# A two-layer attention and gMLP kernel whose instruction order is planned in Python: new priorities, PE transposes, GELU in two ordered halves, scores filled during GELU

## The chip, the cores and the metric

The kernel runs on one core of a Trainium2 chip. The metric is the device time of one execution in microseconds. The core has five engines that each run their own instruction stream in order and meet only at semaphores: TensorE (PE), ScalarE (ACT), VectorE (DVE), GpSimd (POOL) and SyncE (SP), which here only issues DMAs. A wait in a stream holds everything behind it in that stream.

## What is computed

One sequence of S = 2048 tokens of width D = 512 goes twice through two residual blocks:

```python
x = A_x
x = x + A(layernorm(x));  x = x + B(layernorm(x))     # layer 0
x = x + A(layernorm(x));  x = x + B(layernorm(x))     # layer 1, same weights

def A(x):                       # 32 query heads of 16, one shared key/value head
    q = (x @ wq) as 32 heads of 16;  k = x @ wk;  v = x @ wv
    p = softmax(q @ k.T * 16 ** -0.5)
    return (p @ v, heads side by side) @ wo

def B(x):                       # gMLP: F = 1792, half of it 896
    z = gelu(x @ w_in)                       # tanh approximation
    z1, z2 = z[:, :896], layernorm(z[:, 896:])
    g = w_sp @ z2 + b_sp[:, None]            # mixes over the 2048 positions
    return (z1 * g) @ w_out
```

B needs z2 of all positions before its last sum over positions is complete, and layer 1 needs keys and values of all positions of layer 0. So each layer ends in a stretch in which no softmax work is left to fill the engines.

## The kernel before

**Blocks and units.** The softmax exponentials are the bulk: 2 layers x 2048 blocks of 128 keys x 512 (query, head) columns. Query tokens are taken in six chunks, `chunks = [512, 512, 512, 256, 128, 128]`. A group is 512 (query, head) columns for four sets of heads; a unit is a group and one tile of 128 keys, and it has four blocks. PE makes a block's scores (line 1615), ScalarE or VectorE takes the exponential, and PE multiplies the result with the values and adds over the 16 units of a group (line 1419), strictly unit after unit.

**Two engines for the exponential.** ScalarE takes blocks in activations of three and two (line 1343) from a ring of five PSUM banks, `ring = [(0, 3), (3, 2)]`: `FillStream` refills one part of the ring while ScalarE reads the other. VectorE takes single blocks from two further PSUM banks, the side banks 5 and 7, which all other matmul work shares. `DexStream.take` picks such a block at least `LOOK = 6` units ahead of the fill, if a side bank is free and VectorE's queue holds at most `BACKLOG = 3.0` us. Its first operation (line 1520) reads the bank; when two blocks are together, `chain` runs six more (lines 1547 to 1558) and writes the result `Pd`. `PVStream` cannot pass a unit before all its four blocks are done, and the 15 slots of `Pa` that ScalarE writes come free only as `PVStream` goes on.

**The planner.** `Sched` is a list scheduler that runs in Python before anything is built. Each operation has an engine, a modelled duration, dependencies and a priority (a lower number goes first). At each step the engine that can start soonest commits the ready operation of the best priority, and the order of commits becomes the fixed order of that engine's instructions. Streams (fill 0.0, PV 0.5, warm matmuls) compete with ordinary operations. A `job` is matmul work that holds a side bank from its first piece until its readers are done. On the chip the order stays; only the moments differ from the plan.

**The rest of the work.** When a chunk's attention is done, `finish_group` normalises it, `project` transposes it (by DMA, or on PE for the last chunk) and multiplies it with `wo`, `ln` normalises the rows, and `mixer_chunk` computes z1 and z2, stages both without GELU, and then runs GELU on whole staged tiles, so that ScalarE changes its function table twice per batch and not twice per tile. Chunks 0 and 1 share one such batch; 2, 3 and 4 have their own; the last chunk takes GELU straight from PSUM. After GELU come the statistics of z2 (line 1013), an inverse root on GpSimd (1019) and the normalisation (1023).

**Spatial passes.** `passes = [(0, 8, 1), (8, 12, 2), (12, 15, 4)]`: the sum over positions is taken in three passes of 28 jobs (line 1088) as soon as chunks 1, 2 and 4 are through, added into `gp` by VectorE (1100, 1101). The last of these is called the early pass below. The last tile of positions is added in `closing`, which also multiplies by z1 and by `w_out`, and in layer 0 makes the keys of layer 1.

**Warm matmuls.** `WarmStream` issues matmuls of zeros (line 1601) where the planned matmul work in a window of time is small. They wait for nothing but their zero tile and, at times, a bank.

Of the kernel before, what the change touches and what calls it, by code (L numbers as in the profile page):

```python
# [19 lines left out]
FH = 896  # L20
NF = 7
# [11 lines left out]
class Op:  # L33
    __slots__ = ("eng", "fn", "dur", "deps", "prio", "seq", "start", "end", "vis", "sem", "val",
                 "clock", "job", "first", "nun", "users", "ready", "alts", "table", "lat", "dma", "at_commit", "cols", "slow")
# [22 lines left out]
class Sched:  # L58
# [3 lines left out]
    def __init__(self, side_banks):  # L62
# [10 lines left out]
        self.exp_next = None  # L73
        self.tick = {}
# [40 lines left out]
    def op(self, eng, fn, dur, deps=(), prio=5.0, sem=None, job=None, first=False, alts=(), table=None,  # L115
# [28 lines left out]
        o.at_commit = None  # L144
        o.nun = 0
# [20 lines left out]
    def _pick(self, eng):  # L166
# [3 lines left out]
        for o in self.ready[eng]:  # L170
# [8 lines left out]
            if r < INF:  # L179
                cands.append((r, o.prio, o.seq, o, 0.0))  # L180
# [39 lines left out]
    def commit(self, o, t, eng=None):  # L220
# [36 lines left out]
        if o.dma:  # L257
            self.dma_free = max(self.dma_free, o.end) + o.dma / 240e3
            o.vis = self.dma_free + 1.9
# [20 lines left out]
    def job(self, pieces, cons, deps, prio, sem="side", piece_deps=None, soft=()):  # L280
# [3 lines left out]
        for i, (fn, dur) in enumerate(pieces):  # L284
            dd = list(deps) if i == 0 else [prev]
            if piece_deps is not None:
                dd += piece_deps[i]
            prev = self.op("pe", (lambda e, fn=fn: fn(e, j.bank.idx)), dur, dd, prio if i == 0 else min(prio, CONT), sem=sem, job=j,
                           cols=dur * 1900.0, first=(i == 0), soft=[d for c in cons for d in c.get("deps", ())] + list(soft) if i == 0 else ())
        outs = []  # L290
# [74 lines left out]
LOOK = 6  # L365
BACKLOG = 3.0
# [47 lines left out]
class Kern:  # L414
    def __init__(self, nc, A_x, A_wq, A_wk, A_wv, A_wo, B_x, B_w_in, B_w_sp, B_b_sp, B_w_out, out):
# [10 lines left out]
        self.passes = [(0, 8, 1), (8, 12, 2), (12, 15, 4)]  # L426
        self.s_fin = 15
# [79 lines left out]
        sc.streams["pe"] = [self.fill_s, self.pv_s, WarmStream(self)]  # L507
        sc.streams["act"] = [self.exp_s]
        sc.exp_next = self.exp_s.next_time
        self.units = []  # L510
# [23 lines left out]
    def transpose(self, out, src, deps, sem, pr):  # L534
        return self.dma(lambda e: e.dma_start_transpose(out, src), deps, sem, 131072, pr, issue=1.25)
# [265 lines left out]
    def finish_group(self, g, pv_last):  # L801
# [19 lines left out]
        def nm(h, e, b):  # L821
# [16 lines left out]
            [ev, self.c_id], 1.2)  # L838
# [11 lines left out]
    def project(self, g, norms):  # L850
# [7 lines left out]
        for h in range((nq + 1) // 2):  # L858
# [16 lines left out]
            if g.ci < len(self.chunks) - 1:  # L875
# [8 lines left out]
                norms + [self.c_id], 1.3)  # L884
# [4 lines left out]
        for qt in range(nq):  # L889
            t = g.t0 // 128 + qt  # L890

            def pe(e, b, qt=qt):
# [7 lines left out]
                dur=d_psum(512), prio=0.8, deps=[self.x_op[t]])], [evs[qt], self.l_wo], 1.4)  # L900
# [5 lines left out]
    def mixer_chunk(self, g):  # L906
# [5 lines left out]
        pr = PR_LAST if last else (PR_SMALL if g.ci >= 3 else 3.0)  # L912
        evs = []
        war = list(self.xnTB_read)
        for i in range(0, nt, 2):
            ts = T[i:i + 2]
            evs += self.ln(ts, lambda t: [self.x_op[t]], self.xnTB[:, i:i + len(ts), :, :], war, pr, last)
# [29 lines left out]
        elif g.ci == 0:  # L947

            z1v = self.gp[:, 0].bitcast(BF16)
            z1_war = [o for f in range(NF) for o in self.gp_read[(0, f)]]  # L950
        else:
            z1v = self.z1s[:].rearrange("p (f t) -> p f t", f=NF)[:, :, 0:n]
            z1_war = list(self.z1s_free)
# [26 lines left out]
        if g.ci == 0:  # L980
            self.held = (T, z1, z2, z1v)
            return
        zs = [(T[0], n, z1v)]
        if g.ci == 1:
            T, z1, z2 = [a + b for a, b in zip(self.held[:3], (T, z1, z2))]
            zs = [(T[0], n, self.held[3])] + zs
# [4 lines left out]
        def gl(e):  # L991
            for (_t, _n, v) in zs:
                e.activation(v, v, ACTF.Gelu_apprx_tanh)
# [4 lines left out]
        else:  # L998
            gs = z1 = [sc.op("act", gl, d_gelu(NF * nt * 128) + d_gelu(nt * FH), z1 + z2, -1.0, table="gelu")] * (2 * nt)
        for (zt, zn, v) in zs:  # L1000
# [5 lines left out]
            elif zt == 0:  # L1006
                for f in range(NF):
                    self.gp_read[(0, f)] = [sp]
            else:
                self.z1s_free = [sp]  # L1010
# [21 lines left out]

    z2_op = {}
    z2_read = {}
    z1_spill = []
    gp_ops = {}
    gp_read = {}


    def spatial(self, s0, s1, layer):  # L1040
        sc = self.sc
        acc = s0 > 0
        pr = 2.5 if acc else 4.0
        nst = s1 - s0
        early = s1 == self.s_fin
        z2f = self.z2n[:].rearrange("p t f -> p (t f)")
# [18 lines left out]
        nsl = 1 if nst > 4 else 2  # L1065
        for tc in range(4):
            if early:
                w_, ld, held = self.wsP[tc]
            else:
                sl = tc % nsl  # L1070
                w_ = wsl[:, 2048 * sl:2048 * sl + 512 * nst].rearrange("p (s t) -> p s t", s=nst)
                ld = self.dma(lambda e, w_=w_, tc=tc: e.dma_start(w_, self.ws_dv[:, s0:s1, tc * 512:(tc + 1) * 512]),
# [595 lines left out]
```

## Time and profile before

| | |
|---|---|
| median of 8 runs | 1869.98 us (1869.2 to 1872.5) |
| the profiled execution | 1869.83 us, of which the span of instructions is 1868.0 us |
| granted TensorE clock, mean | 0.99 |
| ScalarE busy | 1756.3 us (94% of the span) |
| VectorE busy | 1737.8 us (93%) |
| TensorE busy | 1581.5 us (85%) |
| first exponential of layer 0, last | 14.4 us, 880.6 us |
| last exponential of layer 1 | 1813.0 us |

Times in the profile are microseconds from the start of the span. In a timeline, a row gives start, length, engine, line, operation, tiles, the number of instructions merged into the row, and in brackets the idle time of the engine before it and what ended it. Instructions of one engine overlap a little, so lengths can add up to more than the span.

### The profile page before, as it was taken

What the parts mean: (1) busy time and instruction counts of PE and PEld (TensorE: products, weight loads), DVE (VectorE), ACT (ScalarE), POOL (GpSimd) and SP (SyncE); (2) the same over time, 40 slices, a digit from 0 to 9 for tenths busy, and PEclk for the clock granted to TensorE, in tenths of its full rate; (3) what the DMA queues carried; (4) which work ended last, traced back from release to release, by engine and by line L of the source; (5) the groups of instructions that cost most, each with busy time, mean ns of one, the idle gap of its engine ahead of it and who ended that gap; (6) DMA issues with size and microseconds to landing.
All of it is one profiled execution on the core that took longest, in us unless ns stands there. A gap on an engine that the chain in (4) does not pass through costs nothing.

```text
span 1868.0 us, 30304 instructions
## 1 busy us (share of the span) xinstructions
PE 1581.5 (85%) x11807; PEld 477.6 (26%) x11889; DVE 1737.8 (93%) x3107; ACT 1756.3 (94%) x1581; POOL 53.3 (3%) x94
## 2 busy tenths in 40 slices
PE   8777788778879888989887788887788798998888
PEld 3222222212222222223432122222222222222234
DVE  8999999999889999996889999999999689989978
ACT  8999999999989999998579999999999899999983
POOL 2000000000000000000100000000000000000000
PEclk9999999999999999999999999999999899999999
DMA  9700010000010020221210000000000100111213
GB/s 276 192 1 1 12 35 1 1 1 18 7 40 24 23 46 1 66 72 46 66 33 1 1 1 12 10 26 1 5 14 7 40 24 24 46 43 35 62 45 110
DMA packets 125142, 68.58 MB, mean 37 GB/s; under 512 B 79172, under 2 KB 121416, under 8 KB 125000
## 3 DMA queue, kind: packets, MB, share of 16 engines
q1 hardware_dynamic: 123416, 66.48, 13.2%
q8 instruction: 95, 1.56, 0.3%
q14 instruction: 47, 0.39, 0.1%
q10 hardware_dynamic: 1584, 0.16, 0.1%
HBM read 30.97 MB, written 17.83 MB: 26 GB/s over the span
## 4 chain that ended last, share of the span: by engine, by line
ACT 38%; DVE 27%; PE 18%; issue 15%; POOL 1%; ACTq 0%; POOLq 0%; DVEq 0%
ACT Pa L1343 36%; PE ps_all L1088 5%; PE ps_all L1615 5%; DVE E L1520 4%; DVE Pd L1558 4%; PE ps_all L1419 3%; DVE E L1553 2%; DVE E L1556 2%; DVE E L1547 2%; PE ps_all L1177 2%; DVE gp L1100 2%; DVE st L622 1%; DVE z2n L937 1%; DVE E L1550 1%; DVE E L1549 1%
## 5 line engine op out<-in xcount | busy, mean ns | idle before, releaser
L1343 ACT ACTIVATE Pa<-ps_all 128x1536 bf16<-128x1536 f32 (+1 forms) x1439 | 1637.2, 1371 | 31.8 <-PE ps_all L1615 17.0
L1615 PE MATMUL ps_all<-qs,kT 32*128 32x512 bf16 x4096 | 566.1, 387 | 229.9 <-ACT Pa L1343 207.9
L1520 DVE TENSOR_SCALAR E<-ps_all 128x512 int32<-128x512 f32 x501 | 341.8, 684 | 27.4 <-PE ps_all L1615 24.7
L1615 PEld LDWEIGHTS ps_all<-qs,kT 32*128 32x128 bf16 x4096 | 139.4, 91 | 778.2 <-ACT Pa L1343 726.4
L1419 PE MATMUL ps_all<-Pa,V 128*32 128x512 bf16 x3595 | 325.1, 388 | 1.5 <-DVE Pd L1558 0.6
L1558 DVE SCALAR_TENSOR_TENSOR Pd<-E 128x1024 uint16<-128x1024 int32 x251 | 304.9, 1215 | 1.1
L1601 PE MATMUL ps_all<-zero 128*128 128x512 bf16 x817 | 262.7, 393 | 2.5 <-POOL zero L585 1.0
L1088 PE MATMUL ps_all<-wsT,z2n 128*128 128x512 bf16 x659 | 185.5, 382 | 12.6 <-issue 3.8
L1419 PE MATMUL ps_all<-Pd,V 128*32 128x512 bf16 x501 | 177.7, 389 | 0.0
L1553 DVE TENSOR_TENSOR E<-E 128x1024 f16<-128x1024 f16 x251 | 171.7, 684 | 3.4
L1556 DVE TENSOR_TENSOR E<-E 128x1024 f16<-128x1024 f16 x251 | 171.4, 683 | 2.5
L1547 DVE TENSOR_SCALAR E<-E 128x1024 f16<-128x1024 uint16 x251 | 171.5, 684 | 1.6
L1549 DVE TENSOR_SCALAR E<-E 128x1024 f16<-128x1024 f16 x251 | 105.0, 418 | 2.2
L1550 DVE TENSOR_SCALAR E<-E 128x1024 f16<-128x1024 f16 x251 | 104.6, 417 | 2.3
L1601 PEld LDWEIGHTS ps_all<-zero 128*128 128x128 bf16 x817 | 62.8, 98 | 138.7 <-issue 116.9
L1419 PEld LDWEIGHTS ps_all<-Pa,V 128*32 128x32 bf16 x3595 | 65.4, 94 | 125.1 <-issue 113.8
L1100 DVE TENSOR_TENSOR gp<-ps_all,gp 128x512 f16<-128x512 f32 x112 | 75.1, 683 | 23.2 <-PE ps_all L1088 21.8
L1088 PEld LDWEIGHTS ps_all<-wsT,z2n 128*128 128x128 bf16 x714 | 54.5, 97 | 105.2 <-issue 54.7
L784 PE MATMUL ps_all<-xnTA,wq_pad 128*128 128x512 bf16 (+2 forms) x384 | 72.4, 313 | 2.0 <-DVE qs L793 1.3
L962 PE MATMUL ps_all<-xnTB,w_in_r 128*128 128x512 bf16 (+2 forms) x336 | 62.6, 310 | 5.2 <-DVE z1s L973 2.3
L926 PE MATMUL ps_all<-w_in_r,xnTB 128*128 128x448 bf16 x256 | 63.4, 356 | 3.7 <-DVE z2n L937 1.4
L1013 DVE BATCH_NORM_STATS2 st<-z2n 128x6 f32<-128x448 bf16 x64 | 36.2, 602 | 22.1 <-ACT z2n L994 18.9
(87 smaller groups left out, 1028.3 us busy)
## 6 DMA issues: line engine op xcount, KB each, us to landing
wsT_scratch<-gp SPq DMA_DIRECT2D x16, 512.0 KB, 3.6
wsT<-wsT_scratch SPq DMA_DIRECT2D x8, 1024.0 KB, 5.4
z1s<-z_scratch SPq DMA_DIRECT2D x16, 448.0 KB, 3.8
wsT<-wsT_scratch SPq DMA_DIRECT2D x8, 512.0 KB, 3.4
z_scratch<-z1s SPq DMA_DIRECT2D x4, 896.0 KB, 5.2
X<-in_A_x_dram SPq DMA_DIRECT2D x8, 256.0 KB, 5.6
out_dram<-X SPq DMA_DIRECT2D x16, 128.0 KB, 1.9
w_in_r<-in_B_w_in_dram SPq DMA_DIRECT2D x1, 1792.0 KB, 10.6
```

Of the source, the lines that this page charges most:

```text
L1088: ins = e.matmul(self.b32(b), self.z2n[:, s, f * 128:(f + 1) * 128], w_[:, s - s0, :], start=st, stop=sp)
L1343: return e.activation(k.Pa[:, base:base + n, :], k.b32(b0, n).rearrange("p (k q) -> p k q", k=n), ACTF.Exp, scale=SCALE)
L1419: ins = e.matmul(k.b32(k.pvb)[32 * j:32 * j + 32, :], k.V[:, u.kt, 32 * j:32 * j + 32], b.slot, tile_position=(0, 32 * j), start=u.first, ...
L1520: return k.sc.op("dve", lambda e: e.tensor_scalar(k.eI[:, s, 512 * i:512 * (i + 1)], k.b32(j.bank.idx)[:, 0:512], C_LOG2, C_BIAS, op0=ALU. ...
L1547: return lambda e: e.tensor_scalar(out, a, m, None, op0=ALU.mult)
L1549: return lambda e: e.tensor_scalar(out, a, b, None, op0=ALU.add)
L1550: return lambda e: e.tensor_scalar(out, a, m, b, op0=ALU.mult, op1=ALU.add)
L1553: o4 = sc.op("dve", lambda e: e.tensor_tensor(q, u, w, ALU.mult), d_sb(n, 0.521e-3), [o3], pr)
L1556: o6 = sc.op("dve", lambda e: e.tensor_tensor(q, q, u, ALU.mult), d_sb(n, 0.521e-3), [o5], pr)
L1558: o7 = sc.op("dve", lambda e: e.scalar_tensor_tensor(po.bitcast(U16), I, 2.0 ** -9, q, op0=ALU.mult, op1=ALU.add), d_sb(n, 1.042e-3), [o6] ...
L1601: return e.matmul(k.b32(k.pvb if b is None else b.idx), k.zero[:], k.zero[:, None, :].to_broadcast([P, 4, P]), start=b is not None, stop=b ...
L1615: return e.matmul(self.b32(bank), self.kT[32 * j:32 * j + 32, kt * 128:(kt + 1) * 128], self.qs[32 * j:32 * j + 32, g.q.slot, :], tile_pos ...
```

## The change

1. **Near units first on VectorE.** Operations of VectorE's exponentials carry their unit. If it is less than `NEAR = 4` units ahead of the PV stream, the planner gives them priority 0.1 in place of 2.0 or 2.8.
2. **Spatial.** The early pass gets priority 1.6 (was 2.5), below the 2.0 of `closing`; the adds of a pass never go under 1.0. While one of its jobs waits for its start, `take` gives VectorE no block. `take` also holds back where free side banks would not be enough for waiting jobs of priority under `URGENT = 1.0`. (A split load for passes of more than eight tiles is added too, which the passes here do not use.)
3. **Chunks 3 to 5.** Their transposes and projection get priority 0.9 (were 1.2 to 1.4). For chunk 4 the two DMA transposes (of the attention output and of the normalised rows) become PE transposes with a copy out of PSUM; the last chunk did so already.
4. **GELU.** Chunks 3 and 4 share one batch. In each batch z2 is done first, as its own operation, and z1 after it; the statistics of z2 wait for the first alone, the spill of z1 to DRAM for the second.
5. **`SoloStream`.** A new PE stream at priority 0.4: when both parts of the ring are full and ScalarE is busy for at least 1.2 us more, it makes a single score block for VectorE.
6. **Warm matmuls** that the plan sets after a gap of more than 0.3 us on PE get a wait for the latest ScalarE or VectorE operation that the plan has finished in the 1.5 us before.
7. **Model.** A DMA transpose is planned with 1.2 us of issue and 0.9 us of latency (were 1.25 and 1.9).

```diff
+NEAR = 4
+URGENT = 1.0
+        self.gelus = [(0, 1), (2,), (3, 4), (5,)]
-        sc.streams["pe"] = [self.fill_s, self.pv_s, WarmStream(self)]
+        sc.streams["pe"] = [self.fill_s, self.pv_s, SoloStream(self), WarmStream(self)]
+        sc.unit_now = lambda: self.pv_s.u
...
@@ Sched._pick
-                cands.append((r, o.prio, o.seq, o, 0.0))
+                late = o.unit is not None and o.unit < self.unit_now() + NEAR
+                cands.append((r, 0.1 if late else o.prio, o.seq, o, 0.0))
...
@@ Kern.transpose
-        return self.dma(lambda e: e.dma_start_transpose(out, src), deps, sem, 131072, pr, issue=1.25)
+        return self.sc.op("sp", lambda e: e.dma_start_transpose(out, src), 1.2, deps, pr, sem=sem, dma=131072, lat=0.9)
...
@@ finish_group, project
-            [ev, self.c_id], 1.2)
+            [ev, self.c_id], 0.9 if g.ci >= 3 else 1.2)
-            if g.ci < len(self.chunks) - 1:
+            if g.ci < 4:
-                norms + [self.c_id], 1.3)
+                norms + [self.c_id], 0.9 if g.ci >= 3 else 1.3)
-                dur=d_psum(512), prio=0.8, deps=[self.x_op[t]])], [evs[qt], self.l_wo], 1.4)
+                dur=d_psum(512), prio=0.8, deps=[self.x_op[t]])], [evs[qt], self.l_wo], 0.9 if g.ci >= 3 else 1.4)
...
@@ mixer_chunk
-            evs += self.ln(ts, lambda t: [self.x_op[t]], self.xnTB[:, i:i + len(ts), :, :], war, pr, last)
+            evs += self.ln(ts, lambda t: [self.x_op[t]], self.xnTB[:, i:i + len(ts), :, :], war, pr, last, g.ci == 4)
...
-        def gl(e):
+        def gl1(e):
+            ins = None
             for (_t, _n, v) in zs:
-                e.activation(v, v, ACTF.Gelu_apprx_tanh)
+                ins = e.activation(v, v, ACTF.Gelu_apprx_tanh)
+            return ins
+
+        def gl2(e):
             return e.activation(z2f[:, t0 * FH:(t0 + nt) * FH], z2f[:, t0 * FH:(t0 + nt) * FH], ACTF.Gelu_apprx_tanh)
...
-            gs = z1 = [sc.op("act", gl, d_gelu(NF * nt * 128) + d_gelu(nt * FH), z1 + z2, -1.0, table="gelu")] * (2 * nt)
+            gs = [sc.op("act", gl2, d_gelu(nt * FH), z1 + z2, -1.0, table="gelu")] * (2 * nt)
+            z1 = [sc.op("act", gl1, sum(d_gelu(NF * zn) for _t, zn, _v in zs), z1 + z2, -0.9, table="gelu")]
...
@@ spatial
-        pr = 2.5 if acc else 4.0
+        pr = 1.6 if early else 2.5 if acc else 4.0
...
-                    fn=ev_fn, dur=d_psum(512), prio=pr - 1.5,
+                    fn=ev_fn, dur=d_psum(512), prio=max(1.0, pr - 1.5),
...
+                if early:
+                    self.early_first.append(sc.first_op)
...
@@ DexStream.take
+        if any(o.start is None and o.ready is not None and o.ready <= t for o in k.early_first):
+            return None
+        want = sum(o.first and o.prio < URGENT and o.ready <= t for o in sc.ready["pe"])
+        if want and sum(not b.busy and not b.closed and b.free_at <= t for b in sc.banks) <= want:
+            return None
...
@@ SoloStream.peek
+            t = max(f, sc.bank_free())
+            if not all(k.fill_s.pending) or t == INF or sc.free["act"] < t + 1.2:
+                return None
+            self.x = k.dx_s.take(t, ())
...
+        return (max(f, sc.bank_free(), max(d.vis for d in self.deps)), 0.4)
...
@@ WarmStream.commit
-        o = k.sc.op("pe", fn, 512 / 2400.0, [k.c_zero] + (b.rel if b is not None else []), 9.0, sem="warm")
+        pace = []
+        if t > k.sc.free["pe"] + 0.3:
+            pace = [d for en in ("act", "dve") for d in k.sc.order[en][-8:] if t - 1.5 < d.vis <= t]
+            pace = sorted(pace, key=lambda d: -d.vis)[:1]
+        o = k.sc.op("pe", fn, 512 / 2400.0, [k.c_zero] + pace + (b.rel if b is not None else []), 9.0, sem="warm")
```

## The prediction

> **What bounds it now.** I read the page's busy times and groups first, then ScalarE's own waits, then the timeline around the places where those waits are.
>
> ```profile
> PE 1581.5 (85%) x11807; PEld 477.6 (26%) x11889; DVE 1737.8 (93%) x3107; ACT 1756.3 (94%) x1581; POOL 53.3 (3%) x94
> ...
> L1343 ACT ACTIVATE Pa<-ps_all 128x1536 bf16<-128x1536 f32 (+1 forms) x1439 | 1637.2, 1371 | 31.8 <-PE ps_all L1615 17.0
> ...
> L1520 DVE TENSOR_SCALAR E<-ps_all 128x512 int32<-128x512 f32 x501 | 341.8, 684 | 27.4 <-PE ps_all L1615 24.7
> ```
>
> ScalarE and VectorE share the exponentials and both are nearly full. VectorE does 501 of the 4096 blocks, ScalarE 3595, in 1637.2 us: 0.455 us a block, and that is the price of any block that goes from one to the other. A VectorE block costs 0.684 us for line 1520 and half of a chain (0.684 + 0.418 + 0.684 + 0.417 + 0.683 + 1.215 = 4.10 us): 2.73 us. In windows of 25 us, ScalarE is busy all 25 of 25 through nearly all of 100 to 500 and 975 to 1440: nothing can be gained there unless VectorE takes more. What remains is ScalarE's idle time (112 us) and its work other than exponentials (119 us). Its waits, in total, times and longest:
>
> ```profile
> ACT Pa L1343 <- PE ps_all L1615: 17.0, 41, 1.3
> ACT xnTB L662 <- PE ps_all L654: 13.3, 2, 6.8
> ACT Pa L1343 <- PE ps_all L1419: 13.3, 5, 6.6
> ```
>
> The third is the odd one: exponentials that wait for the PV matmuls, so for free slots of Pa. ScalarE's timeline shows where:
>
> ```profile
> 503.70 1.28 ACT L993 ACT_TABLE_LOAD   x1
> 504.99 3.19 ACT L993 ACTIVATE gp<-gp 128x3584 bf16<-128x3584 bf16 x1
> 508.09 3.17 ACT L993 ACTIVATE z1s<-z1s 128x3584 bf16<-128x3584 bf16 x1
> 511.17 6.16 ACT L994 ACTIVATE z2n<-z2n 128x7168 bf16<-128x7168 bf16 x1
> 517.35 1.28 ACT L1343 ACT_TABLE_LOAD   x1
> 518.64 5.61 ACT L1343 ACTIVATE Pa<-ps_all 128x1024 bf16<-128x1024 f32 x5
> ...
> 538.99 3.28 ACT L1343 ACTIVATE Pa<-ps_all 128x1024 bf16<-128x1024 f32 x3 [3.93 <-PE ps_all L1419]
> ```
>
> and VectorE's timeline over the same stretch why:
>
> ```profile
> 506.67 1.22 DVE L1558 SCALAR_TENSOR_TENSOR Pd<-E 128x1024 uint16<-128x1024 int32 x1
> 517.36 1.68 DVE L1013 BATCH_NORM_STATS2 st<-z2n 128x6 f32<-128x448 bf16 x3 [9.47 <-ACT z2n L994]
> ...
> 533.08 3.47 DVE L1023 TENSOR_SCALAR z2n<-z2n,mv,rs 128x896 bf16<-128x896 bf16 x8 [0.77 <-POOL rs L1019]
> ...
> 539.99 1.23 DVE L1558 SCALAR_TENSOR_TENSOR Pd<-E 128x1024 uint16<-128x1024 int32 x1
> ```
>
> VectorE runs dry for 9.47 us while ScalarE does GELU, z1 first; then statistics and normalisation (priority 2.7 and 2.5) go ahead of the chain (2.8) whose first block was read at 520.4. Its Pd comes after 537.7, the PV matmuls stand until then, and ScalarE stands 3.93 us. Layer 1 repeats it: 9.40 us dry, then 6.59 us of ScalarE at 1477. PE shows the third part:
>
> ```profile
> 504.61 7.30 PE L1601 MATMUL ps_all<-zero 128*128 128x512 bf16 x33
> 519.72 0.61 PE L1615 MATMUL ps_all<-qs,kT 32*128 32x512 bf16 x3 [7.82 <-ACT Pa L1343]
> ```
>
> The 33 warm matmuls, which wait for nothing, run at once; PE then idles 7.82 us, and from 519.7 to 523.9 the granted clock is 0.52, a matmul 0.61 us in place of 0.39.
>
> **The change, term by term** (both layers; minus is time saved).
>
> *A. Waits after the large GELU.* In layer 0 ScalarE idles 0.33 + 3.93 + 0.58 us after it, in layer 1 0.77 + 0.50 + 6.59 + 0.21: 12.9 us, of which 10.5 are the two PV waits. Near-first lifts the chain to 0.1 when its unit is within four of PV. Four units are 16 blocks, some 14 of them ScalarE's, 6.4 us by 0.455; a chain needs 4.1 us plus one operation in its way, so it comes in time. Statistics also start when the z2 half ends, 6.2 us sooner. The stall goes to bn_stats and line 1023, later by a chain of 4.1 us each; behind them waits pass 0, whose adds run until 753, so nothing is late by it. I take 9.5 of the PV waits and 1 of the 2.4 us that the slow clock causes (pacing): **-10.5** (between -5, if the split alone helps, and -12.9).
>
> *B. One GELU batch fewer a layer.* It removes two table loads a layer. A load is 1.28 us, and the next exponential starts 0.01 us after it ends (517.35 + 1.28 against 518.64): 4 x 1.28 = **-5.1**. [...] The rows show no gap on either side of a load (the exponential before it ends at 503.68), so I keep 5.1. The GELU elements are the same, but the two tiles of chunk 3 now come between GELU and the early pass: 1.6 us more z2 GELU, four statistics at 0.60 and two normalisations at 0.51, some 5 us. Against that, chunk 4 reaches its GELU sooner (E).
>
> *C. Scores during GELU.* VectorE's two dry stretches total 18.9 us. What the earlier statistics do not use SoloStream can fill, and either way VectorE time is freed: 18.9 / 2.73 = 6.9 blocks, at 0.455 us 3.1 us. I take 5.5 blocks, since a free bank and a short queue are needed: **-2.5** (0 to -3.1).
>
> *D. After chunk 4's GELU.* ScalarE idles 1.14 us at 860 and 1.30 + 0.24 at 1795, with PE at half clock (0.61 us matmuls, mean clock 0.78 over 854 to 861). Paced warm matmuls keep the clock: **-1.5** (0 to -2.7).
>
> *E. The end of a layer.* From the last exponential to the last chunk's transposed rows:
>
> ```profile
> 880.57 1.28 ACT L1359 ACT_TABLE_LOAD   x1
> ...
> 891.61 0.60 ACT L662 ACTIVATE xnTB<-ps_all 128x512 bf16<-128x512 bf16 x1 [6.56 <-PE ps_all L654]
> ```
>
> and on VectorE between the links of that chain:
>
> ```profile
> 889.52 1.28 DVE L1100 TENSOR_TENSOR gp<-ps_all,gp 128x512 f16<-128x512 f32 x2
> 890.72 0.40 DVE L637 TENSOR_SCALAR xn<-X,mv,rs 128x512 bf16<-128x512 bf16 x1
> 891.03 1.28 DVE L1100 TENSOR_TENSOR gp<-ps_all,gp 128x512 f16<-128x512 f32 x2
> ```
>
> The adds of the early pass still run between the links. The links themselves (PV 0.6, oT 0.69, transposes 0.4, reciprocal 0.25, on 0.42, transposes 0.4, copy 0.6, four matmuls 1.04, X 0.69, statistics 0.68 + 0.17 + 0.14, root 0.6, xn 0.41, transposes 0.4) are 7.5 us, with some 0.1 us for each of 13 hand-overs 8.8. They take 11.0 here and 12.1 in layer 1 (1813.0 to 1825.1), so at most 5.5 us could go if the early pass were over by then. But from 860 to 881 PE is busy 20.3 of 21 us with no warm matmul, and 15 of 28 jobs are done: it is the matmuls that limit the pass, not a priority. It would have to start earlier. PE transposes save some 1.3 us twice (a DMA transpose lands 2.5 us after issue; four PE transposes 0.4 and the copy 0.6 with a semaphore on each side), and held-back banks some 4 us of the 18.8 that chunk 4 takes from its row of X (832.4) to GELU (851.2); the 5 us of B and a shorter attention take that back. **0** (-5.5 to +4, if the pass is that much later). [...]
>
> *F. What it costs.* take() is shut while the early pass waits, and where chunks 3 to 5 want a bank. Line 1520 has 19 blocks from 775 to 860 in layer 0 and none after; 22 from 1700 to 1793. If 8 of these 41 fall to ScalarE: 8 x 0.455 = **+3.6** (0 to +18.7). Four copies more out of PSUM, 0.6 us each, half on ScalarE: **+1.2**. And in the 17 us that A, B and D remove, VectorE would have done 501/1868 blocks a us, 4.6 in all: **+2.1**.
>
> Sum: -10.5 - 5.1 - 2.5 - 1.5 + 0 + 3.6 + 1.2 + 2.1 = -12.7. The span goes from 1868.0 to 1855.3, the execution from 1869.83 to 1857.1; the median lies 0.15 above that execution, so **1857**. This case alone runs from 1850 to 1865.
>
> **Rivals.** *Larger gain:* A in full (12.9), no block lost and E at its best: -12.7 - 2.4 - 3.6 - 5.5 = -24.2, **1846**. For it: four parts of the change aim at the banks and the chain. Against: full PE before the end. *It does not do what it says:* the side banks are always taken, SoloStream never fires, and near-first seldom decides; A falls to -5 and C to 0: -4.7, **1865**. *The gain goes to VectorE's lost share:* all 41 blocks of F move to ScalarE, +15.0 more: **1872**. VectorE's queue there is full of adds, which speaks for it; that only banks with waiting jobs are held back, against. *Slower:* the pacing waits. A paced warm matmul stands in PE's stream; if its VectorE partner is later on the chip than in the plan, the fill behind it waits, and ScalarE with it. A score matmul that waited for a VectorE bank lost 0.44 us (4.4 us over 10 times). It makes the kernel slower once 12.7 + 3.7 = 16.4 us are lost, at 37 such holds; 60 of the 817 warm matmuls give +26.4, **1883**. Against it: most steady-state gaps on PE end with ScalarE, which keeps its planned pace.
>
> **How the numbers follow.** Chances: the sum 0.52, larger gain 0.20, does not do what it says 0.08, lost share 0.10, pacing 0.10. A measurement can tell about 0.2%, 3.7 us: faster is below 1866.2, slower above 1873.7. Faster: 0.51 + 0.20 + 0.05 + 0.02 = 0.78. Same: 0.01 + 0.03 + 0.05 = 0.09. Slower: 0.03 + 0.10 = 0.13. The range for eight in ten, 1842 to 1873, holds nearly all of the first case, 0.15 of the second (E or C may give still more), 0.08 and 0.07.
>
> **What would show it.** A: no wait of line 1343 for line 1419 above 1.5 us, statistics about 6 us after GELU begins. B: 17 table loads in place of 21. C: VectorE idle under 4 us in the large GELU, and line 1520 still at 490 to 510 blocks; under 470 means the lost share. D: clock 0.95 or more right after GELU. E: still 9 to 13 us from the last exponential to the copy of xnTB. Pacing: idle time of ScalarE before line 1343 above 32 us in the steady stretches. The forecast is wrong if the new plan moves stalls to places where ScalarE was full.

## The result and the profile after

The changed kernel takes **1858.8 us** (median of 11 runs, 1853.4 to 1868.1) against 1870.95 for the kernel before (32 runs, 1869.2 to 1878.2): ratio **0.9935, interval 0.9924 to 0.9946**, faster by 0.65%. The profiled execution took 1858.5 us with a span of 1856.7; before it was 1869.83 and 1868.0, so the two spans differ by 11.3 us and can be taken apart.

The page of the changed kernel first: busy time of each engine, then its two groups of exponentials.

```profile
PE 1581.2 (85%) x11779; PEld 474.6 (26%) x11868; DVE 1735.8 (93%) x3108; ACT 1751.1 (94%) x1577; POOL 48.0 (3%) x90
...
L1371 ACT ACTIVATE Pa<-ps_all 128x1536 bf16<-128x1536 f32 (+1 forms) x1439 | 1635.8, 1367 | 24.0 <-PE ps_all L1697 22.3
...
L1554 DVE TENSOR_SCALAR E<-ps_all 128x512 int32<-128x512 f32 x500 | 340.9, 684 | 32.1 <-PE ps_all L1697 29.8
```

VectorE does 500 blocks, before it did 501; ScalarE's exponentials last 1635.8 us, before 1637.2. So the share of the engines hardly moved, and the gain is not more work on VectorE. ScalarE's idle time before exponentials fell from 31.8 to 24.0 us, and its other work by 3.8 (1751.1 - 1635.8 = 115.3, against 119.1). Its waits (engine, what it wants, whom it waits for: us in total, times, longest):

```profile
ACT Pa L1371 <- PE ps_all L1697: 22.3, 43, 3.1
ACT xnTB L671 <- PE ps_all L663: 13.7, 2, 7.0
...
ACT Pa L1371 <- PE ps_all L1447: 0.2, 1, 0.2
```

The wait for the PV matmuls (line 1447, before 1419) is gone: 0.2 us in place of 13.3. The wait for scores (line 1697, before 1615) grew from 17.0 to 22.3. The table loads, before (first two rows) and after (five more loads lie on other lines in each kernel: 21 and 17 in all):

```profile
L993 ACT ACT_TABLE_LOAD x8 | 10.3, 1283 | 0.1
L1343 ACT ACT_TABLE_LOAD x8 | 10.3, 1283 | 0.1
...
L1007 ACT ACT_TABLE_LOAD x6 | 7.7, 1283 | 0.1
L1371 ACT ACT_TABLE_LOAD x6 | 7.7, 1283 | 0.1
```

ScalarE's timeline over the large GELU of layer 0:

```profile
498.95 1.28 ACT L1007 ACT_TABLE_LOAD   x1
500.25 6.18 ACT L1007 ACTIVATE z2n<-z2n 128x7168 bf16<-128x7168 bf16 x1
506.33 3.17 ACT L1003 ACTIVATE gp<-gp 128x3584 bf16<-128x3584 bf16 x1
509.41 3.17 ACT L1003 ACTIVATE z1s<-z1s 128x3584 bf16<-128x3584 bf16 x1
512.60 1.28 ACT L1371 ACT_TABLE_LOAD   x1
513.89 12.45 ACT L1371 ACTIVATE Pa<-ps_all 128x1024 bf16<-128x1024 f32 x11
527.30 2.52 ACT L1371 ACTIVATE Pa<-ps_all 128x1536 bf16<-128x1536 f32 x2 [0.95 <-PE ps_all L1697]
530.80 10.51 ACT L1371 ACTIVATE Pa<-ps_all 128x1536 bf16<-128x1536 f32 x9 [0.98 <-PE ps_all L1697]
```

VectorE over the same stretch:

```profile
505.24 1.29 DVE L1554 TENSOR_SCALAR E<-ps_all 128x512 int32<-128x512 f32 x2 [0.31 <-PE ps_all L1697]
506.45 0.68 DVE L1591 TENSOR_TENSOR E<-E 128x1024 f16<-128x1024 f16 x1
507.05 1.67 DVE L1027 BATCH_NORM_STATS2 st<-z2n 128x6 f32<-128x448 bf16 x3
...
515.98 0.67 DVE L815 CAST oT<-ps_all 128x512 bf16<-128x512 f32 x1
...
516.69 1.17 DVE L1593 SCALAR_TENSOR_TENSOR Pd<-E 128x1024 uint16<-128x1024 int32 x1
```

Two blocks are filled during the GELU (505.24, `SoloStream`), the statistics start 6.8 us after the z2 half begins, and VectorE is idle for 0.31 us where it was 9.47. The chain's last operation, at 516.69, goes between casts and normalisations. PE shows what was left over:

```profile
512.75 1.25 PE L1679 MATMUL ps_all<-zero 128*128 128x512 bf16 x5 [0.79 <-DVE st L1027]
514.97 0.39 PE L1697 MATMUL ps_all<-qs,kT 32*128 32x512 bf16 x2 [0.97 <-ACT Pa L1371]
...
525.76 0.95 PE L1113 MATMUL ps_all<-wsT,z2n 128*128 128x512 bf16 x2
526.64 0.61 PE L1697 MATMUL ps_all<-qs,kT 32*128 32x512 bf16 x3
527.18 1.03 PE L1113 MATMUL ps_all<-wsT,z2n 128*128 128x512 bf16 x2
```

The warm matmuls now come in small groups, each behind a VectorE operation, and the scores right after the GELU run at full clock (0.39 us; clock 1.00 from 513 to 525; in the kernel before the 12 us after this GELU, 518.6 to 530.6, had 0.78). But from 525.9 PE is at half clock after all (0.61 us a score matmul, clock 0.66 from 525 to 530), just when the spatial pass puts its matmuls ahead of the scores: the two waits of 0.95 and 0.98. The largest wait for scores of the kernel, after chunk 2's GELU in layer 0, comes behind spatial matmuls too (line 1113), at the end of a half-clock stretch (clock 0.50 from 730.7 to 737.5):

```profile
739.86 5.97 ACT L1371 ACTIVATE Pa<-ps_all 128x1536 bf16<-128x1536 f32 x5 [3.15 <-PE ps_all L1697]
```

The largest after chunks 3 and 4 comes behind warm matmuls, at half clock as well (0.50 from 853.6 to 856.9); on PE:

```profile
853.00 0.39 PE L1697 MATMUL ps_all<-qs,kT 32*128 32x512 bf16 x2 [4.03 <-ACT Pa L1371]
853.33 3.40 PE L1679 MATMUL ps_all<-zero 128*128 128x512 bf16 x8
856.65 0.74 PE L1697 MATMUL ps_all<-qs,kT 32*128 32x512 bf16 x5
```

PE stood still for 4.03 us, then eight warm matmuls at 0.42 us each ran in front of the scores, and ScalarE idled 2.02 us until 857.23.

**The account of the span.** A layer's attention is counted from its first exponential to its last. Layer 0: 866.2 before, 864.7 after. Layer 1: 893.8 and 882.3. What lies around them is 1.6 us longer: -1.5 - 11.5 + 1.6 = -11.4, the 11.3 of the spans but for rounding. In the attention the parts are, both layers: idle before exponentials -7.8, table loads -5.1, exponentials -1.4, GELU -0.4, other work and its waits +1.6, which is the -13.0 of the two layers but for rounding. In layer 0 the idle time even grew (12.2 to 14.1), since scores came late elsewhere, the 3.15 us at 739.86 above all: nearly all of the gain is in layer 1.

### The profile page after: what moved, and what is told of

Same layout as the page of the kernel before. It is cut to its first block, busy times and chain, and to the rows that moved or that the text cites. A ratio compares the mean times of both kernels' runs of the same rounds, so it can differ in the third digit from the quotient of the medians.

```text
span 1856.7 us, 30131 instructions
## 1 busy us (share of the span) xinstructions
PE 1581.2 (85%) x11779; PEld 474.6 (26%) x11868; DVE 1735.8 (93%) x3108; ACT 1751.1 (94%) x1577; POOL 48.0 (3%) x90
## 4 chain that ended last, share of the span: by engine, by line
ACT 37%; DVE 25%; PE 22%; issue 14%; POOL 1%; DMA 0%; SPq 0%; ACTq 0%; POOLq 0%
ACT Pa L1371 35%; PE ps_all L1697 6%; PE ps_all L1113 5%; DVE E L1554 4%; PE ps_all L1447 4%; DVE Pd L1593 3%; DVE E L1588 2%; DVE E L1591 2%; DVE E L1582 2%; PE ps_all L1679 2%; DVE st L631 1%; PE ps_all L1205 1%; DVE E L1585 1%; DVE E L1584 1%; PE ps_all L936 1%
## 5 line engine op out<-in xcount | busy, mean ns | idle before, releaser
L1371 ACT ACTIVATE Pa<-ps_all 128x1536 bf16<-128x1536 f32 (+1 forms) x1439 | 1635.8, 1367 | 24.0 <-PE ps_all L1697 22.3
L1554 DVE TENSOR_SCALAR E<-ps_all 128x512 int32<-128x512 f32 x500 | 340.9, 684 | 32.1 <-PE ps_all L1697 29.8
L1593 DVE SCALAR_TENSOR_TENSOR Pd<-E 128x1024 uint16<-128x1024 int32 (+1 forms) x251 | 304.2, 1212 | 0.7
L1679 PE MATMUL ps_all<-zero 128*128 128x512 bf16 x780 | 258.1, 402 | 27.9 <-DVE E L1554 3.6
L1113 PE MATMUL ps_all<-wsT,z2n 128*128 128x512 bf16 x650 | 190.6, 388 | 13.3 <-issue 4.3
L1588 DVE TENSOR_TENSOR E<-E 128x1024 f16<-128x1024 f16 (+1 forms) x251 | 171.4, 683 | 3.2
L1591 DVE TENSOR_TENSOR E<-E 128x1024 f16<-128x1024 f16 (+1 forms) x251 | 171.3, 683 | 2.4
L1582 DVE TENSOR_SCALAR E<-E 128x1024 f16<-128x1024 uint16 (+1 forms) x251 | 171.4, 683 | 1.6
L1585 DVE TENSOR_SCALAR E<-E 128x1024 f16<-128x1024 f16 (+1 forms) x251 | 104.9, 418 | 2.6
L1584 DVE TENSOR_SCALAR E<-E 128x1024 f16<-128x1024 f16 (+1 forms) x251 | 104.6, 417 | 2.4
L1205 PE MATMUL ps_all<-E 128*128 128x512 bf16 x215 | 52.1, 380 | 4.2 <-ACT E L1184 1.6
```

Source lines behind the costliest of these rows:

```text
L1113: ins = e.matmul(self.b32(b), self.z2n[:, s, f * 128:(f + 1) * 128], w_[:, s - s0, :] if s - s0 < na or not spare else wsp[:, s - s0 - na, :],
L1371: return e.activation(k.Pa[:, base:base + n, :], k.b32(b0, n).rearrange("p (k q) -> p k q", k=n), ACTF.Exp, scale=SCALE)
L1554: c = k.sc.op("dve", lambda e: e.tensor_scalar(k.eI[:, s, 512 * i:512 * (i + 1)], k.b32(j.bank.idx)[:, 0:512], C_LOG2, C_BIAS, op0=ALU.mul ...
L1582: return lambda e: e.tensor_scalar(out, a, m, None, op0=ALU.mult)
L1584: return lambda e: e.tensor_scalar(out, a, b, None, op0=ALU.add)
L1585: return lambda e: e.tensor_scalar(out, a, m, b, op0=ALU.mult, op1=ALU.add)
```

## The experiments

Each was timed in 5 rounds against the kernel before on the same chip. For differences from the changed kernel I take the difference of the two ratios times 1871 us, as not all ran on one chip.

### One part taken out of the change

**Near units not lifted.** `-NEAR = 4` / `+NEAR = -100000`.

> The changed kernel with NEAR set so low that no VectorE operation is ever lifted; all else as changed. Theory of the prediction (near-first clears the two PV waits of 3.9 and 6.6 us): they come back, line 1371 waits for line 1447 for 5 to 10 us in all, and the time is 5 to 8 us above the changed kernel, some 1864 to 1867 us. Rival (the GELU order does it: with z2 first the statistics are through before the chains are needed): under 2 us above the changed kernel, no wait for line 1447 above 1.5 us.

1871.25 us, ratio 0.9999 (0.9987 to 1.0012): the whole gain is gone, 12 us, more than the theory's 5 to 8. Its waits of exponentials:

```profile
ACT Pa L1371 <- PE ps_all L1697: 23.7, 45, 3.1
ACT Pa L1371 <- PE ps_all L1447: 11.0, 3, 6.7
```

The PV waits are back at 11.0 us, with the z2 half still first. But 6.69 of them come at 655 to 662, in the spatial pass and not after the large GELU: a cast of the pass, four residual adds of a chunk (line 908), two reads of new blocks and links of a second chain come between the links of the first, which takes from 651.95 to 660.93, 9.0 us in place of the 4.1 of its own work. So the lift matters outside the large GELU too.

**z1 first again.** The two priorities of the GELU halves exchanged:

```diff
-  gs = [sc.op("act", gl2, ..., -1.0, table="gelu")] ...
-  z1 = [sc.op("act", gl1, ..., -0.9, table="gelu")]
+  gs = [sc.op("act", gl2, ..., -0.9, table="gelu")] ...
+  z1 = [sc.op("act", gl1, ..., -1.0, table="gelu")]
```

> The changed kernel with the two GELU operations of a batch the other way round, z1 first, so that the statistics of z2 wait for both again. Theory of the prediction: VectorE has some 6 us less to do in each large GELU, 2 to 3 us slower than the changed kernel, near-first still clears the PV wait. Rival (the order is the main gain): 6 to 10 us slower, with PV waits back on ScalarE.

1867.38 us, ratio 0.9980 (0.9970 to 0.9991), so 8.4 us lost, with no PV wait above 0.8 us: the size of the rival, without the PV waits that it named. Neither expectation is met.

**Chunk 3's GELU by itself.** `-gelus = [(0, 1), (2,), (3, 4), (5,)]` / `+gelus = [(0, 1), (2,), (3,), (4,), (5,)]`.

> The changed kernel with chunks 3 and 4 in GELU batches of their own again: 21 table loads, not 17. Theory of the prediction (1.28 us a load): 5.1 us slower than the changed kernel. [...] Rival (waiting for chunk 4 and the longer way to the early pass eat the loads up): within 2 us of the changed kernel or faster.

1869.27 us, ratio 0.9985 (0.9973 to 0.9997): 9.4 us lost where four loads account for 5.1. The trace shows next to nothing beside the 1.28 us of a load: in all 20 loads between other work of ScalarE the load starts 0.02 us after the instruction before it and the next starts 0.01 us after the load. The profiled execution is one of the fastest of its runs (1861.0 at a mean clock of 0.990); the changed kernel took 1853.4 and 1854.3 at that clock, so some 7 us remain.

**Warm matmuls without the wait.** `-if t > k.sc.free["pe"] + 0.3:` / `+if False:`.

> The changed kernel with warm matmuls that wait for nothing, as before. Theory of the prediction: 2 to 3 us slower, with the clock at about half for some 4 us after each large GELU. Rival 1 (the pacing waits hold fills back): faster than the changed kernel by over 3 us. Rival 2 (SoloStream's matmuls and the shorter dry stretch keep the clock already): within 1 us.

1859.08 us, ratio 0.9943 (0.9931 to 0.9955): not to be told from the changed kernel. The theory's 2 to 3 us are not there; the second rival has the time right but not the reason, since without the waits the clock is low (0.59 from 513 to 525). Without them 21 warm matmuls run in one row at 501 and PE then idles 8.28 us. The windows view (window, its length, busy time and number of instructions of each engine, granted clock, DMA) shows the clock of the changed kernel:

```profile
513.00:525.00 12.00, 8.35 (x64) 2.33 (x63) 11.46 (x27) 11.99 (x11) 3.15 (x2) 1.00 0.46 153
525.00:530.00 5.00, 5.00 (x23) 0.94 (x21) 4.00 (x8) 3.80 (x4) 0.00 (x0) 0.66 0.00 0
```

and of the one without the wait:

```profile
513.00:525.00 12.00, 10.83 (x60) 2.31 (x60) 10.30 (x25) 11.04 (x10) 3.15 (x2) 0.59 0.43 143
525.00:530.00 5.00, 4.97 (x38) 1.37 (x36) 4.93 (x10) 4.73 (x5) 0.00 (x0) 1.00 0.02 3
```

So pacing moves the half-clock stretch, but ScalarE waits no less with it: 0.95 + 0.98 = 1.93 us in the 18 us after the load, against 0.51 + 0.24 + 0.22 + 0.21 = 1.18 without.

**No filling during GELU.** `-[self.fill_s, self.pv_s, SoloStream(self), WarmStream(self)]` / `+[self.fill_s, self.pv_s, WarmStream(self)]`.

> The changed kernel without SoloStream. Theory of the prediction: VectorE's share in the large GELUs falls by about 2 blocks a layer, 1 to 2.5 us slower than the changed kernel. Rival (the lone score matmuls only move blocks that VectorE would take a little later): within 1 us.

1863.24 us, ratio 0.9953 (0.9941 to 0.9965): 3.4 us lost, a little over the theory's 1 to 2.5. VectorE still does 501 blocks, so the blocks it misses in the GELU it takes elsewhere. ScalarE's idle time before exponentials is 32.2 us in place of 24.0, of which 3.1 are waits for the PV matmuls, the longest 2.2.

**Nothing refused to VectorE, no urgent early pass.** The two early returns in `take` out, and `-pr = 1.6 if early else 2.5 if acc else 4.0` / `+pr = 2.5 if acc else 4.0`.

> The changed kernel with take() never shut for waiting jobs and the early pass at 2.5 again; the priorities 0.9 of the jobs of chunks 3 to 5 stay. Theory of the prediction (the refusals cost blocks and give nothing back): line 1554 has 505 to 510 blocks, 2 to 4 us faster than the changed kernel. Rival (the banks they keep free bring chunk 4 to its GELU sooner and the early pass with it): slower by 2 to 6 us, GELU of chunk 4 some 4 us later.

1857.22 us, ratio 0.9924 (0.9903 to 0.9944), overlapping that of the changed kernel; 505 blocks in place of 500. The refusals cost VectorE five blocks, 5 x 0.455 = 2.3 us, and in these two traces they are paid back at the end: from the last exponential to the end it took 59.0 us here, 55.5 with them. The theory's 505 blocks are there; its 2 to 4 us cannot be told from nothing.

**Chunk 4's transposes by DMA again.** `-if g.ci < 4:` / `+if g.ci < 5:`, and the fifth chunk's flag to `ln` dropped.

> The changed kernel with chunk 4's two transposes done by DMA again. Theory of the prediction (2.5 us of slack hides them): within 2 us of the changed kernel. Rival (chunk 4 is on the path to the early pass and so to the end of the layer): 3 to 5 us slower, the last exponential to xnTB over 13 us.

1868.66 us, ratio 0.9982 (0.9972 to 0.9993): 8.8 us lost, more than either expectation. Yet chunk 4 reaches its GELU no later: the load comes 35.5 us before layer 1's last exponential, in the changed kernel 33.8. VectorE has 493 blocks, and waits 42.5 us for their scores in place of 29.8; ScalarE's exponentials take 1641.0 us (+5.2) and its idle time before them is 28.5 (+4.5). Why is not shown.

Seven parts taken out one at a time cost 12.0 + 8.4 + 9.4 + 1.5 + 3.4 - 2.1 + 8.8 = 41.4 us; the whole change gained 12.2. Either the parts need one another, or each edit makes the planner write another order and pays for that too.

### An edit that means nothing

`-"dve": 0.14` / `+"dve": 0.15`, the hand-over latency that the planner counts for VectorE; once in the changed kernel, once in the kernel before.

> The changed kernel with one number of the planner altered that means nothing for the work: VectorE's hand-over latency counted as 0.15 us instead of 0.14, so that the written order of the engines differs while every rule of the change stays. Theory 1 (the leave-one-out runs are steep because each part really carries its gain): within 2 us of the changed kernel, 1857 to 1861. Theory 2 (any edit draws a new order from a spread of some 5 us, and the changed order is a good draw): 3 to 10 us slower, 1862 to 1869, with other small waits for scores after the GELUs and no PV wait above 2 us.

> The kernel before with the same meaningless number altered (0.15 for 0.14). Theory 1: within 2 us of the kernel before, and the two PV waits after the large GELU return (8 to 12 us in sum). Theory 2: 3 to 8 us away from it on either side; PV waits still there, since nothing lifts the chain over the statistics, but of another size.

Changed kernel: 1864.16 us, ratio 0.9963 (0.9950 to 0.9975), **5.2 us slower** than with 0.14. Kernel before: 1875.69, ratio 1.0022 (1.0009 to 1.0034), **4.1 slower**. Theory 2 has the times right: a new order is worth some 4 to 5 us by itself, and no difference below that says anything of a part. Its signs are missed in part: the changed kernel with 0.15 has a PV wait of 2.7 us (3.0 in all), and VectorE does 493 blocks in it too, so the transposes are not needed for that number.

The pair still differs by 1875.69 - 1864.16 = 11.5 us, as the first pair did by 12.1, so the change is faster under both orders, but not in the same way. The traces of the second pair differ by 6.0 us (spans of 1870.1 and 1864.1): the four loads give 5.1, idle time before exponentials 1.7 (29.0 and 27.3), since the PV waits that A removes are not there. And the runs of this pair have mean clocks of 0.981 and 0.990, those of the first 0.988 and 0.984. By 0.9 us for each 0.001 (last section) some 8 of the second pair's 11.5 us go with the clock, an estimate; at equal clocks it would differ by some 3 us, and the first pair by some 15. The mean clock is a part of what an order draws. What the change gains is therefore known to several us only, and what a single part gains cannot be read from its removal to better than about 5 us.

The kernel before with 0.15 holds a second surprise, in its waits:

```profile
ACT Pa L1343 <- PE ps_all L1615: 25.6, 49, 1.5
...
ACT Pa L1343 <- PE ps_all L1419: 1.6, 4, 0.8
```

Nothing lifts the chain, yet the PV waits are 1.6 us and not 13.3. VectorE's timeline in the large GELU of layer 0, first one row of the kernel before, then two of this one:

```profile
520.38 0.69 DVE L1520 TENSOR_SCALAR E<-ps_all 128x512 int32<-128x512 f32 x1
...
522.75 1.68 DVE L1013 BATCH_NORM_STATS2 st<-z2n 128x6 f32<-128x448 bf16 x3 [9.13 <-ACT z2n L994]
...
531.58 0.69 DVE L1520 TENSOR_SCALAR E<-ps_all 128x512 int32<-128x512 f32 x1 [1.53 <-PE ps_all L1615]
```

It is dry for 9.13 us as before, but its next block is first read 7.5 us after the exponentials resume (531.58 against 524.03; in the kernel before 520.38 against 518.64), so its chain was not yet needed while the statistics ran; that this is the reason is argued, the small PV waits are measured. The stall that I priced was an accident of one order. The waits for scores are 25.6 us here, 17.0 there.

### Parts alone, on the kernel before

**The lift alone**, as in the diff of the change (`unit`, `NEAR = 4`, priority 0.1), GELU in one piece. Then **the lift and the z2 half first**. Then these two and **the early pass made urgent** (`pr = 1.6 if early`, adds not under 1.0, `take` shut while it waits).

> The kernel before with the chain's lift alone, GELU still z1 first in one piece. The lift decides term A by itself: VectorE still idles 8 to 9.5 us in each large GELU, statistics start only after it, but the chain comes before them, so PV waits under 2 us and a time of 1862 to 1866. If the earlier statistics are needed too, PV waits of 3 us or more remain and the time is 1867 or above.

> The kernel before with term A alone: the chain's operations lifted when their unit is within four of PV, and the z2 half of GELU first. Nothing else of the change. My sum: -9.5 of the PV waits, less 1.2 that VectorE would have done in that time: 1862 to 1864, with PV waits under 2 us and 21 table loads. Spread theory: the PV waits go all the same, but the time lies anywhere from 1860 to 1871.

The lift alone: 1884.21 us, ratio 1.0069 (1.0057 to 1.0082), **slower than before by 13 us**, with the small PV waits of the first expectation and a time, 17 us above 1867, that only the second one's "or above" covers. With the z2 half first: 1864.34, ratio 0.9961 (0.9948 to 0.9974), faster by 7.3, close to my sum, without any PV wait. The waits of the lift alone:

```profile
ACT Pa L1348 <- PE ps_all L1625: 36.6, 65, 2.1
...
ACT Pa L1348 <- PE ps_all L1424: 0.9, 1, 0.9
```

and of both, where no wait for the PV matmuls is left:

```profile
ACT Pa L1353 <- PE ps_all L1630: 22.4, 44, 1.9
```

The lift took 12.4 us of PV waits away in the first, and waits for scores took 19.6 more. VectorE is still dry for 8.42 us in the large GELU of layer 0 and has its statistics to do afterwards, only later; that this other work, which empties PSUM, is what keeps the scores waiting is argued, not shown. With the statistics under the GELU the same lift leaves 22.4. Of the 14.2 us by which its span is longer (1882.2), 8.4 lie behind the last exponential; and the mean clock of its runs is 0.979 against 0.988 before, some 8 us by the slope of the last section. The two accounts overlap.

But the second does not give what its attention gives. Layer 1 is shorter by 13.8 us (880.0 against 893.8), and then the time from the last exponential to the end is 63.0 us in place of 55.0. On PE, at the end:

```profile
1839.77 0.59 PE L1098 MATMUL ps_all<-z2n 128*128 128x512 bf16 x2
1840.20 2.75 PE L1098 MATMUL ps_all<-wsT,z2n 128*128 128x512 bf16 x12
1843.34 3.20 PE L1187 MATMUL ps_all<-E 128*128 128x512 bf16 x14 [0.39 <-DVE gp L1110]
...
1851.59 2.11 PE L1098 MATMUL ps_all<-wsT,z2n 128*128 128x512 bf16 x9
```

Matmuls of the spatial passes (line 1098) stand between those of `closing` 40 to 54 us after the last exponential, and ScalarE idles 13.27 us there. Of the passes' adds 32 were left at the last exponential, before 14, and came due at the end. VectorE had taken 510 blocks, nine more than before; that they put the adds off is argued.

> The kernel before with the chain's lift, the z2 half first, and the early pass made urgent (priority 1.6, its adds 1.0, no VectorE blocks started while it waits). Nothing else of the change: 21 table loads, DMA transposes, no filling during GELU, no paced warm matmuls. In the run with the first two alone the attention of layer 1 ended 13.5 us sooner than before, but 32 adds of the early pass were left then, in place of 14, and the rest of the layer took 63.0 us in place of 55.0. If the urgency of the early pass is what turns the shorter attention into a shorter kernel: under 20 adds left, 55 to 57 us from the last exponential to the end, and 1856 to 1859, the time of the whole change. If the urgency only moves work (blocks refused, attention longer): 55 to 57 us at the end, but the last exponential 5 us or more later, and 1863 to 1867. A drawn order may add 5 us to either.

1863.93 us, ratio 0.9964 (0.9951 to 0.9978): both expectations missed. The attention was as short (879.0), but 28 adds were left and 62.1 us to the end. Urgency does not bring the early pass forward enough, because the middle pass, which adds into the same `gp`, is late. The rows below count the adds of both later passes (56 in layer 1) from the end of chunk 4's last normalisation on, when the data of the early pass are ready: in the kernel before, before with 0.15, lift and z2 first, the same with the early pass urgent, and changed.

```profile
L1100 DVE TENSOR_TENSOR gp<-ps_all,gp x28: 627/691/693, 1794.6 to 1825.1; 128x512 f16<-128x512 f32 x28
L1100 DVE TENSOR_TENSOR gp<-ps_all,gp x28: 626/688/692, 1797.4 to 1828.2; 128x512 f16<-128x512 f32 x28
L1110 DVE TENSOR_TENSOR gp<-ps_all,gp x42: 658/682/693, 1782.5 to 1855.2; 128x512 f16<-128x512 f32 x42
L1113 DVE TENSOR_TENSOR gp<-ps_all,gp x42: 627/684/693, 1783.0 to 1854.1; 128x512 f16<-128x512 f32 x42
L1126 DVE TENSOR_TENSOR gp<-ps_all,gp x35: 628/685/693, 1779.9 to 1827.2; 128x512 f16<-128x512 f32 x35
```

In both kernels before only the 28 adds of the early pass are left then; in the two with parts 14 of the middle pass are to be done first, in the changed kernel 7. Chunk 4's own time is not the cause: its GELU starts 24.4 us before the last exponential in the two with parts, and 24.9 in the kernel before with 0.15, which has 15 adds left. Chunk 4 comes earlier in the changed kernel (33.8) and in the seven reduced ones (32.8 to 37.4), and leaves more time for the same adds. What the changed kernel and all seven have, and the two with parts lack, are the priority 0.9 for chunks 3 to 5 and the planner's shorter latency for DMA transposes; neither was run alone, and why the middle pass is late stays open.

### Where the time lies in each

The median is of all runs of a kernel, the other columns are from its one profiled execution (us; adds are the spatial passes' adds left at layer 1's last exponential):

| kernel | median | attention 0 | attention 1 | last exponential to end | adds left |
|---|---|---|---|---|---|
| before | 1870.95 | 866.2 | 893.8 | 55.0 | 14 |
| before, 0.15 | 1875.69 | 869.2 | 893.1 | 54.7 | 15 |
| lift alone | 1884.21 | 872.2 | 892.0 | 63.4 | 32 |
| lift, z2 first | 1864.34 | 866.1 | 880.0 | 63.0 | 32 |
| the same, early pass urgent | 1863.93 | 867.5 | 879.0 | 62.1 | 28 |
| changed | 1858.84 | 864.7 | 882.3 | 55.5 | 18 |
| changed, 0.15 | 1864.16 | 855.7 | 898.9 | 56.7 | 20 |
| near units not lifted | 1871.25 | 868.7 | 891.2 | 54.9 | 10 |
| z1 first | 1867.38 | 860.9 | 892.9 | 55.4 | 13 |
| chunk 3's GELU alone | 1869.27 | 860.0 | 890.4 | 57.1 | 20 |
| no paced waits | 1859.08 | 860.4 | 887.2 | 55.3 | 18 |
| no filling | 1863.24 | 870.9 | 880.8 | 56.7 | 19 |
| nothing refused | 1857.22 | 861.3 | 883.1 | 59.0 | 22 |
| DMA transposes | 1868.66 | 867.0 | 893.3 | 55.3 | 12 |

Attention 0 ranges over 17 us and attention 1 over 20, and they do not go together: the changed kernel with 0.15 has the shortest layer 0 and the longest layer 1. With up to 18 adds left the end takes 54.7 to 55.5 us; from there on it is longer by 0.5 to 1.3 us for each add.

## Why the prediction was right, and where its steps were not

The forecast was 1857 us, range 1842 to 1873; the time is 1858.8. The two largest terms, A and B, are in the traces at their size. That the sum comes within 2 us is luck in part: idle time outside the stretches of A and D grew by 4.1 us and what lies around the attention by 1.6, neither of them in the sum, while C and F, forecast at +4.4, came to about nothing; and a new order alone moves the time by 4 to 5.

**A, -10.5.** In the stretches that it named (490 to 540 and 1430 to 1500) ScalarE's idle time before exponentials went from 12.4 to 2.4 us: -10.0. No PV wait above 0.2 us, and the statistics came 6.8 us after the GELU began, as named. The Pd that the stall of layer 0 waited for lies between the last two rows shown in the prediction:

```profile
537.67 1.22 DVE L1558 SCALAR_TENSOR_TENSOR Pd<-E 128x1024 uint16<-128x1024 int32 x1
```

That the lift needs the earlier statistics is shown by the two kernels with parts alone (20 us apart), that the earlier statistics need the lift by the changed kernel without it (11.0 us of PV waits); that "the split alone helps" with 5 us was not tried on the kernel before. What the step did not see is that idle time elsewhere grew from 19.4 to 21.6 us, and that the stall is a matter of the order: the kernel before with 0.15 lacks it and is slower.

**B, -5.1.** 17 loads, 5.1 us less of load time in the attention. The rows of the changed kernel show no gap behind a load either (the next exponential starts at 513.89, the load ends at 513.88). That separate batches lost 9.4 us does not show a dearer load: no gap beside the loads is over 0.02 us in that trace, and the 4.3 us above 5.1 lie within what a new order costs (4 to 5).

**C, -2.5, and F, +3.6 with +1.2 and +2.1.** VectorE's dry time went as named (0.31 us). The net of the four was +4.4; the exponentials' time fell by 1.4, ScalarE's other work and waits rose by 1.6. In F's own stretches the loss is about as sized: 41 blocks in the last 113 us of each layer's attention before (in layer 0 the 19 are counted from 767; from 775 there are 17), 35 after, so six fewer where eight were forecast. What the sum lacked is that VectorE takes five others elsewhere: 500 in all against 501, and 505 with nothing refused.

**D, -1.5.** ScalarE's idle before exponentials at 800 to 890 and 1760 to 1830 fell from 4.1 to 2.2 us, all of it in layer 1. In layer 0 the stall itself did not: 1.14 became 2.02, in spite of the pacing. The named sign, a clock of 0.95 or more right after GELU, holds for the large one of layer 0 (1.00) and for layer 1 at 1773 to 1780 (1.00), not at 854 to 861 (0.79; before it was 0.81 there, and not the 0.78 of the prediction). Taking pacing out changed the time by nothing measurable, so its part in D falls.

**E, 0.** From the last exponential to the copy of xnTB 12.3 and 12.2 us, before 11.1 and 12.1: the named 9 to 13. The end is 0.5 us longer. The step "it would have to start earlier" looked at chunk 4 alone and took the middle pass as through, as it is in the kernel before. That need not hold: with parts alone the middle pass was late, 28 to 32 adds were left and the end cost 7 to 8 us. In the changed kernel the attention of layer 1 is 11.5 us shorter, the middle pass is half as far behind, chunk 4 comes some 6 us earlier against the last exponential (33.8 against 27.3), and 18 adds are left. I had priced E as a gain or a loss of its own, and not as the condition for A's.

**The rivals.** Larger gain, no effect and lost share are out for this order (1858.8; 0.2 us of PV waits; 500 blocks). Pacing waits that make it slower are out: idle before exponentials is 24.0 us, not over 32, and without pacing nothing is won. The last sentence, that the forecast is wrong "if the new plan moves stalls to places where ScalarE was full", describes what happened in part: at 600 to 760 in layer 0 idle time went from 2.7 to 5.6, at 1080 to 1300 from 0.9 to 4.1.

What stays open: why the DMA transposes and the z1 order cost 8 to 9 us each, and separate batches some 4 more than their loads. The first two exceed the two orders that were drawn (4 to 5 us), but two draws do not bound the spread, and no stall of that size is in their traces. No kernel here is shown to beat the changed one; the one with nothing refused is level with it.

## What to carry to other kernels

Where a planner writes the order, first measure an edit that means nothing: here it moved the time by 4 to 5 us, as much as several parts of the change, and a stall seen in one order may be absent in the next. Judge a change by pairs under several such edits, with the clock of the runs beside the time, and a part by the row that it should change. When a stall in the main phase is taken away, count what is still to be done when that phase ends: here 32 adds in place of 14 came due in the tail and took 8 of 14 us back.

## What the runs showed of the hardware

The spread between runs of one kernel goes with the granted clock. The changed kernel's runs lie between a mean clock of 0.975 (1868.1 us) and 0.990 (1853.4), about 0.9 us for each 0.001; in the other kernels with six or more runs the slope is 0.6 to 1.2. In the traces of the kernel before and of the changed one every record of the granted clock is 1.00 or 0.50. The stretches at 0.50 are 3.4, 6.8 or 13.7 us long: 6 of them, 37.5 us in sum, in the profiled run before; 11, 47.8 us, in the one after. With the lift alone the profiled run has a mean clock of 0.980 over 1882.2 us, which makes some 75 us at 0.50, an estimate. What sets where the stretches fall and how long they last is not shown. By the slope the change gives some 3 us back: the mean clock of its runs is 0.984, before 0.988.
